# K transposed one batch ahead, P*V late in each step, and the last batch by head groups, in a cached attention kernel on Trainium2

## The chip, the cores and the metric

The kernel runs on one core of a Trainium2 chip. The core has a matrix engine (TensorE, in the profile PE, with its weight loads as PEld), VectorE (DVE), ScalarE (ACT), GpSimd (POOL) and SyncE (SP), which run side by side and wait for one another on semaphores. Data comes from HBM into SBUF by DMA, matmul results land in PSUM, which has eight banks. The metric is the time of one execution in microseconds (us) on the device. The time before is a median of 3 runs.

## What is computed

One attention block with a cache, for 32 sequences (batches) of 4 query tokens each: a query projection, attention of 32 query heads over 4 key/value heads with 2048 cached positions, and an output projection. All inputs are bf16.

```python
B, Sq, D = 32, 4, 1024
Hq, Hkv, Sk, Dh = 32, 4, 2048, 128
q = (x @ wq).reshape(B, Sq, Hq, Dh)            # heads first
k = jnp.repeat(k_cache, rep, axis=1)
v = jnp.repeat(v_cache, rep, axis=1)
scores = jnp.einsum("bhqd,bhkd->bhqk", q, k) * (Dh ** -0.5)
p = _softmax(scores, axis=-1)
o = jnp.einsum("bhqk,bhkd->bhqd", p, v)
return o.reshape(B, Sq, Hq * Dh) @ wo          # heads back beside the tokens first
```

K and V are 2048 KB each for every batch, wq and wo 8192 KB each, so some 151 MB are read from HBM.

## The kernel before

The program is written out by hand as one list of operations for each engine (`p.op`, `p.dma`), each with the names of what it waits for and the name of what it finishes. An engine runs its list strictly in that order, so an operation that waits holds up everything behind it on its engine. All loads are issued by SP, in one list too.

**Start.** x and the four pieces of wq are loaded, then K and V by batch. PE transposes x and makes the projection of all queries (L184), which ACT and DVE copy to `QT_sb`.

**A batch.** K of a batch arrives with its rows over the partitions, and its head dimension must come onto the partitions before the scores can be made. PE transposes it in eight fills of eight 128x128 blocks (`pe_fill`, L216). Each fill goes to one PSUM bank of a ring, and is copied from there to `KT_sb` by DVE (L228) or ACT (L230). PE then makes the scores of the 32 heads (`pe_qk`, L252) into `ps_s`, four banks, 32 rows for each key/value head. DVE takes the maximum (L301) and negates it (L302), ACT takes the exponential and the sum (L306), DVE the reciprocal (L311). PE transposes P in two fills (`pe_pt`, L236), DVE copies them to `PT_sb` (L243). PE multiplies P by V in 64 small matmuls (`pe_pv`, L260), 16 for each of the four head groups, each group in its own 32 columns of the array. ACT scales the result by the reciprocal into `o_sb` (L287), PE transposes it (L291), ACT copies it to `oT_sb` (L295).

**Output.** After every eighth batch PE multiplies eight batches of `oT_sb` by wo in 128 matmuls (`oproj`, L318), DVE copies the result to `y_sb` (L326), and four stores of 16 KB go out (L330), on POOL, and for the last eight batches on SP and ACT.

**Buffers.** K has two buffers (`NKB`), V three (`NVB`), K^T two (`NKTB`). The ring has three PSUM banks (`NRING`), for fills of K and P only; the fourth bank, `ps_o`, is shared by P*V, the transposed output and the output projection, which wait for one another. The load of K of batch b waits for the last fill of batch b-2 (L139), the load of V of batch b for P*V of batch b-3 (L144). V of the last batch comes in four pieces, by head group, and its P*V runs one head group after the other (L281).

**Order of a step.** K is transposed two batches ahead (`AHEAD`). Step i is: scores of i, maximum of i, P*V of i-1 and its evacuation, fills 0 and 1 of batch i+2, transpose of the output of i-1, exponential of i, fills 2 to 7 of batch i+2, in every eighth step the output projection, reciprocal of i, transposes of P of i. Steps 30 and 31 have no fills.

Of the kernel before, what the change touches and what calls it, by code (L numbers as in the profile page):

```python
# [56 lines left out]
def bass_standalone__gqa_block_cached__sampling_kernel(  # L57
# [20 lines left out]
    NKB = 2  # L78
    NVB = 3
    NKTB = 2  # L80
    AHEAD = 2
    NFILL = 8
    TB = T // NFILL
    NRING = 3
# [4 lines left out]
    ACT_FILLS = (0, 1, 5, 7)  # L89
    DVE_FILLS = (2, 3, 4, 6)  # L90
# [4 lines left out]
    with ExitStack() as es:  # L95
# [7 lines left out]
        KT_sb = sbuf("KT_sb", [128, NKTB, TV, G, R * C], BF16)  # L103
# [7 lines left out]
        y_sb = sbuf("y_sb", [128, 2, NC], BF16)  # L111
# [8 lines left out]
        ring = [ps_r[:, i, :].bitcast(BF16) for i in range(NRING)]  # L120
        ps_o = ps_r[:, 3, :]
# [54 lines left out]
        for kt in range(KT):  # L176
            p.op("pe", lambda e, kt=kt: e.transpose(
                ring[2][:, kt * 128:(kt + 1) * 128],
                x_sb.rearrange("p (c a) -> p a c", a=KT)[:, kt, :], ident[:, :]),
                ["x", "ident"], "xT" if kt == KT - 1 else None)  # L180
        p.op("dve", lambda e: e.tensor_copy(xT_sb.rearrange("p a b -> p (a b)"), ring[2]), ["xT"], "xT_evac")
# [18 lines left out]
        ring_evac = []  # L200

        def ring_slot(name):
            n = len(ring_evac)
            waits = [ring_evac[n - NRING]] if n >= NRING else [("qe", 4 + n)]
            ring_evac.append(name)
            return ring[n % NRING], waits

        slot_of = {}

        def pe_fill(b, f):  # L210
            buf, waits = ring_slot(("kt", b, f))
            slot_of["kt", b, f] = buf
            for q in range(TB):
                c, v = q // (TB // C), q % (TB // C)
                t = c * TV + f * TB // C + v
                p.op("pe", lambda e, q=q, t=t: e.transpose(  # L216
                    buf[:, q * 128:(q + 1) * 128], K_sb[:, b % NKB, t, :], ident[:, :]),
                    waits + [("k", b), "ident"] if q == 0 else [], ("fill", b, f) if q == TB - 1 else None)

        def evac(b, f):  # L220
            buf = slot_of["kt", b, f]
            waits = [("fill", b, f)]
            if b >= NKTB:
                waits.append(("qk", b - NKTB))
            dst = KT_sb[:, b % NKTB, f * TB // C:(f + 1) * TB // C, :, :].rearrange("p v g (r c) -> p (v g) r c", c=C)
            src = buf.rearrange("p (c m r) -> p m r c", c=C, r=R)
            if f in DVE_FILLS:
                p.op("dve", lambda e: e.tensor_copy(dst, src), waits, ("kt", b, f))  # L228
            else:
                p.op("act", lambda e: e.activation(dst, src, ACT.Copy), waits, ("kt", b, f))  # L230

        def pe_pt(i, f):
            buf, waits = ring_slot(("pt", i, f))
            slot_of["pt", i, f] = buf
            for q in range(8):
                p.op("pe", lambda e, q=q: e.transpose(  # L236
                    buf[:, q * 128:(q + 1) * 128], P_sb[:, (8 * f + q) * 128:(8 * f + q + 1) * 128], ident[:, :]),
                    waits + [("exp", i)] if q == 0 else [], ("ptf", i, f) if q == 7 else None)

        def evac_pt(i, f):  # L240
            buf = slot_of["pt", i, f]
            waits = [("ptf", i, f)] + ([("pv", i - 1)] if i else [])
            p.op("dve", lambda e: e.tensor_copy(  # L243
                PT_sb[:, 8 * f:8 * f + 8, :].rearrange("p t q -> p (t q)"), buf), waits, ("pt", i, f))


        def pe_qk(i):
            waits = [("kt", i, f) for f in range(NFILL)]
            waits += [("qe", j) for j in range(Hq // 4)] if i == 0 else [("exp", i - 1)]
            for c in range(4):  # L250
                for g in range(G):
                    p.op("pe", lambda e, c=c, g=g: e.matmul(  # L252
                        ps_s[32 * g:32 * (g + 1), c * 512:(c + 1) * 512],
                        lhsT=QT_sb[:, i, REP * g:REP * (g + 1), :],
                        rhs=KT_sb[:, i % NKTB, 4 * c:4 * (c + 1), g, :],
                        start=True, stop=True, tile_position=(0, 32 * g)),
                        waits, ("qk", i) if (c, g) == (3, G - 1) else None)

        def pv_mm(i, g, t, waits, done):
            p.op("pe", lambda e: e.matmul(  # L260
                ps_o[32 * g:32 * (g + 1), 0:Dh],
                lhsT=PT_sb[:, t, 32 * g:32 * (g + 1)],
                rhs=V_sb[:, i % NVB, g, t, :],
                start=(t == 0), stop=(t == TV - 1), tile_position=(0, 32 * g)), waits, done)

        def pe_pv(i):
            waits = [("pt", i, 0), ("pt", i, 1)]
            if i == 0:
                waits.append(("qe", 7))
            else:  # L270
                waits.append(("ot", i - 1))
                if i % OG == 0:
                    waits.append(("oe", i // OG - 1))
            if i < B - 1:
                waits.append(("v", i))
                for t in range(TV):
                    for g in range(G):
                        pv_mm(i, g, t, waits if t == 0 and g == 0 else [],
                              ("pv", i) if (t, g) == (TV - 1, G - 1) else None)
            else:  # L280
                for g in range(G):  # L281
                    for t in range(TV):
                        pv_mm(i, g, t, waits + [("v", i, g)] if t == 0 else [],
                              ("pv", i) if (t, g) == (TV - 1, G - 1) else None)

        def o_evac(i):
            p.op("act", lambda e: e.activation(o_sb[:, :], ps_o[:, 0:Dh], ACT.Copy, scale=rinv[:, i:i + 1]),  # L287
                 [("pv", i), ("rinv", i)] + ([("oT", i - 1)] if i else []), ("o", i))

        def pe_ot(i):  # L290
            p.op("pe", lambda e: e.transpose(ps_o[:, 0:64].bitcast(BF16), o_sb[:, :], ident[:, :]),  # L291
                 [("o", i)], ("oT", i))

        def ot_evac(i):
            p.op("act", lambda e: e.activation(  # L295
                oT_sb[:, :, i * Sq:(i + 1) * Sq],
                ps_o[:, 0:64].bitcast(BF16).rearrange("p (h s) -> p h s", s=Sq), ACT.Copy),
# [16 lines left out]
        def oproj(n):  # L314
            waits = [("wo", c) for c in range(4)] + [("ot", OG * n + OG - 1)]
            for h in range(Hq):
                for j in range(4):
                    p.op("pe", lambda e, h=h, j=j: e.matmul(  # L318
                        ps_o[32 * j:32 * (j + 1), 0:NC],
# [3 lines left out]
                        waits if (h, j) == (0, 0) else [], ("op", n) if (h, j) == (Hq - 1, 3) else None)  # L323

        def oproj_out(n):
            p.op("dve", lambda e: e.tensor_copy(y_sb[:, n % 2, :], ps_o[:, 0:NC]),  # L326
                 [("op", n)] + ([("out", n - 2, j) for j in range(4)] if n >= 2 else []), ("oe", n))
            for j in range(4):
                p.dma("act" if n == NOG - 1 and j % 2 else "sp" if n == NOG - 1 else "pool",
                      lambda e, j=j: e.dma_start(  # L330
                          out_flat[32 * n:32 * (n + 1), NC * j:NC * (j + 1)], y_sb[32 * j:32 * (j + 1), n % 2, :]),
                      [("oe", n)], ("out", n, j), f"s_o{n}{j}")

        for b in range(AHEAD):
            for f in range(NFILL):
                pe_fill(b, f)
                evac(b, f)
        for i in range(B):
            nb = i + AHEAD
            more = nb < B  # L340
# [5 lines left out]
            if more:  # L346
                for f in (0, 1):
                    pe_fill(nb, f)
                    evac(nb, f)
            if i >= 1:  # L350
                pe_ot(i - 1)
                ot_evac(i - 1)
            softmax_exp(i)
            if more:
                for f in range(2, NFILL):
                    pe_fill(nb, f)
                    evac(nb, f)
            if i >= 1 and i % OG == 0:
                oproj(i // OG - 1)
                oproj_out(i // OG - 1)  # L360
            softmax_rinv(i)
# [3 lines left out]
        pe_pv(B - 1)  # L365
        o_evac(B - 1)
        pe_ot(B - 1)
        ot_evac(B - 1)
        oproj(NOG - 1)
        oproj_out(NOG - 1)  # L370

# [55 lines left out]
```

## Time and profile before

| | us |
|---|---|
| time, median of 3 runs | 399.6 |
| lowest and highest run | 398.33, 401.64 |
| the profiled execution, its own time | 398.7 |
| its span, from the first to the last instruction | 396.9 |

The granted clock of TensorE was 0.951 of full speed on average in that execution. The time of an execution is a little longer than its span; durations below are from the span. In the profile, L12 stands for line 12 of the kernel, and a row of a group names engine, line, operation, the tile written and the tile read. "Idle before" is time in which the engine had nothing to run, with the engine or transfer that ended it. The chain of work that ended last is followed back from the last instruction: it shows which waits mattered. The table of stretches gives the busy time of each engine, the granted clock, the share of time in which the 16 DMA engines were busy (it can come out a little over 1) and the rate in GB/s.

### The profile page before, as it was taken

The numbers are of one execution on the slowest core, as the hardware profiler recorded it, in microseconds if no ns is written. First come the engines' busy times: TensorE is split into PE (matmuls) and PEld (weight loads), VectorE is DVE, ScalarE is ACT, GpSimd is POOL, SyncE is SP. The second block draws the span as 40 slices with busy tenths as digits, with TensorE's granted clock in tenths as the row PEclk, the third lists the DMA queues.
The fourth block names the chain that finished last, engine by engine and source line by source line (L and its number), as shares of the span: only waits on it lengthen the run. The fifth ranks groups of instructions, "written<-read, shape, count | busy, mean of one in ns | idle before, by whom it ended". The sixth has DMA issues, their size and how long they took to land.

```text
span 396.9 us, 12651 instructions
## 1 busy us (share of the span) xinstructions
PE 285.8 (72%) x5928; PEld 229.8 (58%) x5928; DVE 274.5 (69%) x297; ACT 207.7 (52%) x261; POOL 6.7 (2%) x18
## 2 busy tenths in 40 slices
PE   2967688466374878887777787877767878876565
PEld 2956466446364656665555575755555756655454
DVE  0017899375383984998888867988888589987520
ACT  1016677245154663676656646766666657666320
POOL 0000000000000002000000010000000010000000
PEclk9999999787888999999999999999999999999858
DMA  8999999999999999999999999999999999999400
GB/s 330 433 423 418 390 408 395 414 409 396 413 412 418 416 418 409 422 415 419 414 414 417 416 417 387 424 414 417 417 418 416 419 400 391 418 418 404 165 0 9
DMA packets 27059, 152.32 MB, mean 384 GB/s; under 512 B 1472, under 2 KB 1792, under 8 KB 22400
## 3 DMA queue, kind: packets, MB, share of 16 engines
q1 hardware_dynamic: 26528, 151.29, 93.5%
q8 instruction: 46, 0.75, 0.8%
q0 software_dynamic: 384, 0.20, 0.2%
q10 hardware_dynamic: 96, 0.03, 0.0%
q14 instruction: 5, 0.04, 0.0%
HBM read 151.26 MB, written 0.26 MB: 382 GB/s over the span
## 4 chain that ended last, share of the span: by engine, by line
DMA 51%; DVE 23%; PE 21%; issue 2%; ACT 1%; SPq 1%
DMA K_sb<-in_k_cache_dram 51%; DVE KT_sb L228 18%; PE ps_r L216 9%; DVE mx L301 4%; PE ps_r L318 4%; PE ps_r L236 3%; PE ps_s L252 3%; PE ps_r L260 2%; ACT P_sb L306 1%; SPq L133 0%; DVE negmx L302 0%; PE ps_r L291 0%; DVE PT_sb L243 0%; DVE y_sb L326 0%; SPq L130 0%
## 5 line engine op out<-in xcount | busy, mean ns | idle before, releaser
L216 PE MATMUL ps_r<-ident,K_sb 128*128 128x128 bf16 x2048 | 150.5, 227 | 86.6 <-DMA K_sb<-in_k_cache_dram 44.1
L216 PEld LDWEIGHTS ps_r<-ident,K_sb 128*128 128x128 bf16 x2048 | 123.7, 101 | 112.4 <-issue 39.1
L228 DVE COPY KT_sb<-ps_r 128x1024 bf16<-128x1024 bf16 x128 | 147.7, 1216 | 53.1 <-PE ps_r L216 53.1
L230 ACT ACTIVATE KT_sb<-ps_r 128x1024 bf16<-128x1024 bf16 x128 | 127.9, 1026 | 67.6 <-PE ps_r L216 67.5
L301 DVE TENSOR_REDUCE mx<-ps_s 128x1 f32<-128x2048 f32 x32 | 73.3, 2292 | 10.1 <-PE ps_s L252 9.6
L306 ACT ACTIVATE P_sb<-ps_s,negmx 128x2048 bf16<-128x2048 f32 x32 | 63.4, 1980 | 1.3 <-DVE negmx L302 1.3
L287 ACT ACTIVATE o_sb<-ps_r,rinv 128x128 bf16<-128x128 f32 x32 | 11.8, 367 | 84.9 <-PE ps_r L260 84.9
L236 PE MATMUL ps_r<-ident,P_sb 128*128 128x128 bf16 x512 | 40.1, 226 | 6.6 <-ACT P_sb L306 6.2
L243 DVE COPY PT_sb<-ps_r 128x1024 bf16<-128x1024 bf16 x64 | 42.2, 690 | 3.1 <-PE ps_r L236 2.2
L260 PEld LDWEIGHTS ps_r<-V_sb,PT_sb 128*32 128x32 bf16 x2048 | 33.8, 98 | 12.1 <-DVE PT_sb L243 10.6
L260 PE MATMUL ps_r<-V_sb,PT_sb 128*32 128x128 bf16 x2048 | 38.9, 222 | 1.8 <-issue 1.0
L236 PEld LDWEIGHTS ps_r<-ident,P_sb 128*128 128x128 bf16 x512 | 30.4, 100 | 13.4 <-ACT P_sb L306 6.4
L252 PE MATMUL ps_s<-KT_sb,QT_sb 128*32 128x512 bf16 x512 | 34.1, 387 | 0.0
L252 PEld LDWEIGHTS ps_s<-KT_sb,QT_sb 128*32 128x32 bf16 x512 | 10.8, 97 | 10.7 <-issue 0.7
L195 DVE CAST QT_sb<-ps_r 128x512 bf16<-128x512 f32 x2 | 1.3, 686 | 22.6 <-PE ps_r L184 22.6
L326 DVE CAST y_sb<-ps_r 128x256 bf16<-128x256 f32 x4 | 1.7, 425 | 20.2 <-PE ps_r L318 20.2
L318 PE MATMUL ps_r<-w_sb,oT_sb 128*32 128x256 bf16 x512 | 14.8, 273 | 0.4 <-ACT oT_sb L295 0.4
L184 PE MATMUL ps_s<-P_sb,w_sb 128*128 128x128 bf16 x128 | 9.8, 237 | 7.1 <-DMA w_sb<-in_wq_dram 7.1
L197 ACT ACTIVATE QT_sb<-ps_r 128x512 bf16<-128x512 f32 x2 | 1.1, 594 | 26.1 <-PE ps_r L184 26.1
L318 PEld LDWEIGHTS ps_r<-w_sb,oT_sb 128*32 128x32 bf16 x512 | 13.2, 97 | 1.3 <-ACT oT_sb L295 0.5
L184 PEld LDWEIGHTS ps_s<-P_sb,w_sb 128*128 128x128 bf16 x128 | 8.6, 107 | 7.7 <-issue 4.4
L330 POOL DMA_DIRECT2D out_dram<-y_sb x12 | 6.0, 507 | 312.4 <-DVE rinv L311 312.4
(20 smaller groups left out, 61.4 us busy)
## 6 DMA issues: line engine op xcount, KB each, us to landing
K_sb<-in_k_cache_dram SPq DMA_DIRECT2D x32, 2048.0 KB, 14.6
V_sb<-in_v_cache_dram SPq DMA_DIRECT2D x31, 2048.0 KB, 19.3
w_sb<-in_wq_dram SPq DMA_DIRECT2D x4, 2048.0 KB, 14.1
w_sb<-in_wo_dram SPq DMA_DIRECT2D x4, 2048.0 KB, 23.6
V_sb<-in_v_cache_dram SPq DMA_DIRECT2D x4, 512.0 KB, 14.6
P_sb<-in_x_dram SPq DMA_DIRECT2D x1, 256.0 KB, 2.7
out_dram<-y_sb POOLq DMA_DIRECT2D x12, 16.0 KB, 6.9
out_dram<-y_sb SPq DMA_DIRECT2D x2, 16.0 KB, 1.7
```

The lines of the kernel that those rows point to most:

```text
L184: p.op("pe", lambda e, kt=kt, h=h: e.matmul(ps_q(h), lhsT=w_sb[:, kt, h * Dh:(h + 1) * Dh], rhs=xT_sb[:, kt, :], start=(kt == 0 and h % 4 ...
L216: p.op("pe", lambda e, q=q, t=t: e.transpose(buf[:, q * 128:(q + 1) * 128], K_sb[:, b % NKB, t, :], ident[:, :]), waits + [("k", b), "iden ...
L228: p.op("dve", lambda e: e.tensor_copy(dst, src), waits, ("kt", b, f))
L230: p.op("act", lambda e: e.activation(dst, src, ACT.Copy), waits, ("kt", b, f))
L236: p.op("pe", lambda e, q=q: e.transpose(buf[:, q * 128:(q + 1) * 128], P_sb[:, (8 * f + q) * 128:(8 * f + q + 1) * 128], ident[:, :]), wai ...
L243: p.op("dve", lambda e: e.tensor_copy(PT_sb[:, 8 * f:8 * f + 8, :].rearrange("p t q -> p (t q)"), buf), waits, ("pt", i, f))
L252: p.op("pe", lambda e, c=c, g=g: e.matmul(ps_s[32 * g:32 * (g + 1), c * 512:(c + 1) * 512], lhsT=QT_sb[:, i, REP * g:REP * (g + 1), :], rh ...
L260: p.op("pe", lambda e: e.matmul(ps_o[32 * g:32 * (g + 1), 0:Dh], lhsT=PT_sb[:, t, 32 * g:32 * (g + 1)], rhs=V_sb[:, i % NVB, g, t, :], sta ...
L287: p.op("act", lambda e: e.activation(o_sb[:, :], ps_o[:, 0:Dh], ACT.Copy, scale=rinv[:, i:i + 1]), [("pv", i), ("rinv", i)] + ([("oT", i - ...
L301: p.op("dve", lambda e: e.tensor_reduce(mx[:, i:i + 1], ps_s[:, :], AX.X, ALU.max), [("qk", i)], ("mx", i))
L306: p.op("act", lambda e: e.activation(P_sb[:, :], ps_s[:, :], ACT.Exp, bias=negmx[:, i:i + 1], scale=scale, accum_out=ssum[:, i:i + 1]), [( ...
L318: p.op("pe", lambda e, h=h, j=j: e.matmul(ps_o[32 * j:32 * (j + 1), 0:NC], lhsT=oT_sb[:, h, 32 * n:32 * (n + 1)], rhs=wo_sb[:, h, NC * j:N ...
```

## The change

* K^T has one buffer, K has three, and K is transposed one batch ahead: the load of K of batch b waits for the last fill of batch b-3. Loads begin with K of 0, 1 and 2, then V of 0; from there K of b+2 stands ahead of V of b.
* The ring has all four banks, and P*V, the transposed output and the output projection take their turn in it. A turn waits for the evacuation of what used its bank four turns ago. DVE copies fills 2, 3, 5 and 7 (before 2, 3, 4 and 6), ACT the others.
* A step runs in another order: scores of i, maximum, transposed output of i-2, the output projection in every eighth step, fills 0 and 1 of i+1, exponential, fills 2 to 7 of i+1, reciprocal, P*V of i-1 and its evacuation, transposes of P of i.
* The last batch runs P*V of its first three head groups interleaved, then of the fourth; evacuates, transposes and projects 24 heads, then 8; and its projection goes to `ps_s`.
* `y_sb` has a place for each of the four groups of eight batches. Stores of the first three groups are issued on SP at the end of its list, ahead of those of the last group.

```diff
-    NKB = 2
+    NKB = 3
-    NKTB = 2
-    AHEAD = 2
-    NRING = 3
+    NRING = 4
-    ACT_FILLS = (0, 1, 5, 7)
-    DVE_FILLS = (2, 3, 4, 6)
+    DVE_FILLS = (2, 3, 5, 7)
...
-        load_v(0)
-        load_k(2)
-        nk = 3
-        for b in range(1, B):
-            if nk < B:
-                load_k(nk)
-                nk += 1
+        for b in range(B):
+            if b + 2 < B:
+                load_k(b + 2)
             load_v(b)
...
+        freed = [("qe", 4 + n) for n in range(NRING)]
+
+        def slot(free):
+            n = len(freed)
+            freed.append(free)
+            return ring[n % NRING], [freed[n - NRING]]
...
-            waits = [("fill", b, f)]
-            if b >= NKTB:
-                waits.append(("qk", b - NKTB))
+            waits = [("fill", b, f)] + ([("qk", b - 1)] if b else [])
...
         def pe_pv(i):
-            waits = [("pt", i, 0), ("pt", i, 1)]
...
+            buf, waits = slot(("o", i))
+            slot_of["o", i] = buf
+            waits = waits + [("pt", i, 0), ("pt", i, 1), ("v", i)]
+            for t in range(TV):
                 for g in range(G):
...
+                    pv_mm(buf, i, g, t, waits if t == 0 and g == 0 else [],
+                          ("pv", i) if (t, g) == (TV - 1, G - 1) else None)
...
+        for f in range(NFILL):
+            pe_fill(0, f)
+            evac(0, f)
         for i in range(B):
             pe_qk(i)
             softmax_max(i)
+            if i >= 2:
+                pe_ot(i - 2)
+                ot_evac(i - 2)
+                if i % OG == 1 and i > 1:
+                    oproj(i // OG - 1)
+            if i + 1 < B:
+                for f in (0, 1):
+                    pe_fill(i + 1, f)
+                    evac(i + 1, f)
+            softmax_exp(i)
+            if i + 1 < B:
+                for f in range(2, NFILL):
+                    pe_fill(i + 1, f)
+                    evac(i + 1, f)
+            softmax_rinv(i)
             if i >= 1:
                 pe_pv(i - 1)
                 o_evac(i - 1)
...
             for f in range(2):
                 pe_pt(i, f)
                 evac_pt(i, f)
...
+        L = B - 1
+        pe_ot(L - 1)
+        ot_evac(L - 1)
+        o_l, waits = slot(None)
+        waits = waits + [("pt", L, 0), ("pt", L, 1)]
+        for t in range(TV):
+            for g in range(3):
+                pv_mm(o_l, L, g, t, waits + [("v", L, k) for k in range(3)] if t == 0 and g == 0 else [],
+                      ("pva", L) if (t, g) == (TV - 1, 2) else None)
+        for t in range(TV):
+            pv_mm(o_l, L, 3, t, [("v", L, 3)] if t == 0 else [], ("pv", L) if t == TV - 1 else None)
...
+        oproj_mm(y_l, n, range(24), ["ota", ("ot", L - 1)], None)
...
+        oproj_mm(y_l, n, range(24, 32), ["otb"], ("op", n))
+        oproj_evac(y_l, n)
+        for m in range(NOG - 1):
+            oproj_out(m, ("sp",))
+        oproj_out(n, ("sp", "act"))
```

More of the change, by code (lines that the diff above doesn't have):

```diff
@@ L119, in bass_standalone__gqa_block_cached__sampling_kernel @@
         ps_r = es.enter_context(nc.psum_tensor("ps_r", [128, 4, 512], F32))
-        ring = [ps_r[:, i, :].bitcast(BF16) for i in range(NRING)]
-        ps_o = ps_r[:, 3, :]
+        ring = [ps_r[:, i, :] for i in range(NRING)]
         def ps_q(h):
@@ L311, in softmax_rinv, with oproj_mm @@
             p.op("dve", lambda e: e.reciprocal(rinv[:, i:i + 1], ssum[:, i:i + 1]), [("exp", i)], ("rinv", i))
-        def oproj(n):
-            waits = [("wo", c) for c in range(4)] + [("ot", OG * n + OG - 1)]
-            for h in range(Hq):
+        def oproj_mm(buf, n, heads, waits, done):
+            for h in heads:
                 for j in range(4):
                     p.op("pe", lambda e, h=h, j=j: e.matmul(
-                        ps_o[32 * j:32 * (j + 1), 0:NC],
+                        buf[32 * j:32 * (j + 1), 0:NC],
                         lhsT=oT_sb[:, h, 32 * n:32 * (n + 1)],
@@ L334, in bass_standalone__gqa_block_cached__sampling_kernel, with oproj, oproj_evac @@
[L334 to L337, printed above, removed]
+                        waits if (h, j) == (heads[0], 0) else [], done if (h, j) == (heads[-1], 3) else None)
+        def oproj(n):
+            buf, waits = slot(("oe", n))
+            oproj_mm(buf, n, range(Hq), waits + [("wo", c) for c in range(4)] + [("ot", OG * n + OG - 1)], ("op", n))
+            oproj_evac(buf, n)
+        def oproj_evac(buf, n):
+            p.op("dve", lambda e: e.tensor_copy(y_sb[:, n, :], buf[:, 0:NC]), [("op", n)], ("oe", n))
@@ L338, in bass_standalone__gqa_block_cached__sampling_kernel, with oproj_out @@
+        def oproj_out(n, engines):
+            for j in range(4):
+                p.dma(engines[j % len(engines)], lambda e, j=j: e.dma_start(
+                    out_flat[32 * n:32 * (n + 1), NC * j:NC * (j + 1)], y_sb[32 * j:32 * (j + 1), n, :]),
+                    [("oe", n)], ("out", n, j), f"s_o{n}{j}")
+        for f in range(NFILL):
+            pe_fill(0, f)
+            evac(0, f)
         for i in range(B):
-            nb = i + AHEAD
-            more = nb < B
             pe_qk(i)
@@ L364, in bass_standalone__gqa_block_cached__sampling_kernel @@
                 evac_pt(i, f)
[L365 to L370, printed above, removed]
+        L = B - 1
[9 more added lines that the diff above has]
+            pv_mm(o_l, L, 3, t, [("v", L, 3)] if t == 0 else [], ("pv", L) if t == TV - 1 else None)
+        p.op("act", lambda e: e.activation(o_sb[0:96, :], o_l[0:96, 0:Dh], ACT.Copy, scale=rinv[0:96, L:L + 1]),
+             [("pva", L), ("rinv", L), ("oT", L - 1)], "oa")
+        p.op("act", lambda e: e.activation(o_sb[96:128, :], o_l[96:128, 0:Dh], ACT.Copy, scale=rinv[96:128, L:L + 1]),
+             [("pv", L)], "ob")
+        ta, waits = slot(None)
+        ta = ta.bitcast(BF16)
+        p.op("pe", lambda e: e.transpose(ta[:, 0:96], o_sb[0:96, :], ident[0:96, 0:96]), waits + ["oa"], "oTa")
+        p.op("dve", lambda e: e.tensor_copy(
+            oT_sb[:, 0:24, L * Sq:(L + 1) * Sq], ta[:, 0:96].rearrange("p (h s) -> p h s", s=Sq)), ["oTa"], "ota")
+        y_l = ps_s[:, 0:512]
+        n = NOG - 1
+        oproj_mm(y_l, n, range(24), ["ota", ("ot", L - 1)], None)
+        tb, waits = slot(None)
+        tb = tb.bitcast(BF16)
+        p.op("pe", lambda e: e.transpose(tb[:, 0:32], o_sb[96:128, :], ident[96:128, 96:128]), waits + ["ob"], "oTb")
+        p.op("dve", lambda e: e.tensor_copy(
+            oT_sb[:, 24:32, L * Sq:(L + 1) * Sq], tb[:, 0:32].rearrange("p (h s) -> p h s", s=Sq)), ["oTb"], "otb")
+        oproj_mm(y_l, n, range(24, 32), ["otb"], ("op", n))
[3 more added lines that the diff above has]
+        oproj_out(n, ("sp", "act"))
         names = list(p.ENGINES) + sorted({s for s in p.dma_count})
```

87 lines of the change are left out of this document (21 added, 66 removed).

## The prediction

> **What bounds the kernel now.** I read the page's head, then its row of GB/s by slice, then the chain of work that ended last by engine.
>
> ```profile
> PE 285.8 (72%) x5928; PEld 229.8 (58%) x5928; DVE 274.5 (69%) x297; ACT 207.7 (52%) x261; POOL 6.7 (2%) x18
> GB/s 330 433 423 418 390 408 395 414 409 396 413 412 418 416 418 409 422 415 419 414 414 417 416 417 387 424 414 417 417 418 416 419 400 391 418 418 404 165 0 9
> DMA 51%; DVE 23%; PE 21%; issue 2%; ACT 1%; SPq 1%
> K_sb<-in_k_cache_dram SPq DMA_DIRECT2D x32, 2048.0 KB, 14.6
> V_sb<-in_v_cache_dram SPq DMA_DIRECT2D x31, 2048.0 KB, 19.3
> ```
>
> No engine is full, yet the DMA rate stands near 417 GB/s from the first slices to the 37th of 40. A batch is one K and one V load, 2 x 2048 KB = 4.19 MB, so at 417 GB/s it takes 10.06 us. The engines need less. In the order-of-time listing of PE after an output projection, where PE waits for no load, one step follows another like this (start, length, engine, line, tile):
>
> ```profile
> 326.98 1.22 PE L236 MATMUL ps_r<-ident,P_sb 128*128 128x128 bf16 x16
> 335.68 1.23 PE L236 MATMUL ps_r<-ident,P_sb 128*128 128x128 bf16 x16
> ```
>
> That is 8.70 us a step. So the kernel has two parts: a stream of loads that sets the pace, and a tail after the last K has landed. The table of stretches (stretch, length, PE, PEld, DVE, ACT, POOL busy, granted clock, DMA share, GB/s) shows how full the stream is:
>
> ```profile
> 60.00:120.00 60.00, 37.37 (x729) 30.98 (x726) 37.20 (x40) 26.22 (x34) 0.00 (x0) 0.83 1.03 406
> 120.00:240.00 120.00, 91.34 (x2041) 72.29 (x2042) 93.40 (x101) 70.11 (x89) 4.05 (x8) 0.99 1.02 417
> 240.00:260.00 20.00, 16.99 (x357) 13.34 (x355) 18.39 (x20) 15.29 (x20) 0.00 (x0) 1.00 1.00 405
> 325.00:330.00 5.00, 4.18 (x113) 3.04 (x112) 4.66 (x7) 2.95 (x4) 0.00 (x0) 1.00 0.89 331
> ```
>
> It is full but for two dents, each a step or so behind an output projection (3.7 us of PE). The first costs 20 x (417-405)/417 = 0.6 us, the second 5 x (417-331)/417 = 1.0 us. The tail is the end of the chain in order of time (start, length, what):
>
> ```profile
> 344.53 14.69 DMA K_sb<-in_k_cache_dram
> 359.35 1.05 PE ps_r L216 x16
> 367.27 2.30 DVE mx L301
> 369.78 2.07 ACT P_sb L306 x2
> 371.89 1.89 PE ps_r L236 x16
> 373.78 1.61 PE ps_s L252 x12
> 375.42 2.30 DVE mx L301
> 377.93 2.07 ACT P_sb L306 x2
> 380.04 1.90 PE ps_r L236 x16
> 381.97 0.70 DVE PT_sb L243
> 382.71 5.68 PE ps_r L260 x61
> 388.42 0.38 ACT o_sb L287
> 389.11 0.28 ACT oT_sb L295
> 389.44 3.71 PE ps_r L318 x128
> 393.17 0.42 DVE y_sb L326
> ```
>
> The last K lands at 344.53 + 14.69 = 359.2; call this T. The span ends at 396.9, so the tail is 37.7 us. It holds the transposes of the last K (for batch 31), a whole softmax of batch 30, a whole softmax of batch 31, P*V, and the output. The second softmax starts only because K was transposed two batches ahead: batch 30's scores come after batch 31's K.
>
> **The change, part by part: the stream.** Bytes and load order stay, but for V of batch 0, which goes behind K of batch 2. With three K buffers, the load of K(b) waits for the transposes of batch b-3 instead of b-2. At the end of step i, with K(i+1) transposed and V(i-1) used, four loads may stand issued behind it: K(i+2), V(i), K(i+3), V(i+1), which is 4 x 5.03 = 20 us. Before, a K load landed 14.6 us after its issue. P*V moves to the end of its step, so V(i+2) is issued later within the step, but behind that 20 us queue it is hidden. Both dents should fill: I take 0.6 + 1.0 = 1.6 us. Bounds: nothing, or 4.5 us if the weak start (390 and 395 GB/s in slices 5 and 7) and the uneven end (165 in the 38th) also level out. A loss of 1 us is left open, since the issue order on SP changes.
>
> **The step.** What could undo this is a longer step. The ACT and PE rows of batch 30's step give the lengths:
>
> ```profile
> 361.97 1.98 ACT L306 ACTIVATE P_sb<-ps_s,negmx 128x2048 bf16<-128x2048 f32 x1
> 363.92 1.04 ACT L230 ACTIVATE KT_sb<-ps_r 128x1024 bf16<-128x1024 bf16 x1
> 365.01 1.22 PE L236 MATMUL ps_r<-ident,P_sb 128*128 128x128 bf16 x16
> 366.17 1.05 PE L252 MATMUL ps_s<-KT_sb,QT_sb 128*32 128x512 bf16 x16
> 367.04 1.06 PE L260 MATMUL ps_r<-V_sb,PT_sb 128*32 128x128 bf16 x64
> ```
>
> The new ring gives 12 slots a step (oT, eight fills, o, two P^T) over four banks, so P*V takes the bank of fill 4, which ACT copies out after the exponential. The new loop is: scores to maximum 1.10 (366.17 to 367.27), maximum to exponential 2.51 (to 369.78), exponential to fill 4's copy 1.95, the copy 1.04, the hand-over 0.15, P*V 1.0, P^T to scores 1.16. The sum is 8.9 us, against 8.70 before and DVE's 274.5/32 = 8.6. It stays under 10.06, so the stream still paces the kernel. P*V also waits for V(i-1), which follows K(i+1) by one transfer (5.0 us); fill 4 is copied 5.75 us after the K landing, so V is hidden with 0.7 us to spare. The projections now stand on PE ahead of the fills and push those back by some 3.6 us; at 10.06 - 8.9 = 1.2 us a step that is made good in three or four steps. The last one is at step 25, and T belongs to step 30. The 20 us queue covers the lag. The second K^T buffer goes without cost, as PE does the scores of i before the fills of i+1 anyway.
>
> **The tail, from T.** In step 30 the first fill starts 0.14 after T, the exponential follows ACT's first two copies, and fill 4's copy ends 363.92 + 1.04 - 359.21 = 5.75 after T. P*V of batch 29 follows to 6.9, P^T to 8.05, where the scores of 31 start (before, scores of 30 started at 7.0). Then 1.10 to the maximum, 2.51 to the exponential, 2.11 to P^T (369.78 to 371.89), 2.63 to its copies' end (380.04 to 382.67): 16.4. P*V of 30 and its transpose fit in the gaps. The last P*V before went head group by head group: 64 in 5.68, or 0.0887 each. Now three groups interleave: 16 rounds bounded by 1.42 (a round costs what one does) and 4.26 (no overlap). The interleaved P*V row (1.06 for 64, 0.066 a round at clock 1.00) is nearer the low end; doubled for the half clock it gives 2.1, so I take 1.8. The fourth group alone costs 16 x 0.0887 = 1.42. That ends at 19.7 with its hand-over. Evacuating the first 96 rows hides behind group four, the last 32 behind the projection. A transpose and a copy follow: 0.24 + 0.36; the copy has no DVE row, and between the 0.28 of ACT's oT copy and the 0.42 of y's I take 0.28 and 0.08 of hand-over. Projection of 24 heads: 96/128 x 3.71 = 2.78. A second transpose and copy: 0.6. Eight heads: 0.93. Copy of y 0.44. From there to the end as before, 396.9 - 393.59 = 3.31. Sum 28.3.
>
> The clock must be added. The last matmul ahead of the last softmax, and PE's busy time, its granted clock, DMA share and GB/s in single microseconds at the end:
>
> ```profile
> 376.73 0.23 PE L291 MATMUL ps_r<-ident,o_sb 128*128 128x128 bf16 x1 [0.48 <-ACT o_sb L287]
> ...
> 371.00:372.00 1.00, 0.11 (x2) 0.78 0.48 188
> 374.00:375.00 1.00, 1.00 (x16) 0.52 0.00 0
> 378.00:379.00 1.00, 0.00 (x0) 0.69 0.00 0
> 387.00:388.00 1.00, 1.00 (x14) 0.50 0.00 0
> 388.00:389.00 1.00, 0.54 (x5) 0.69 0.00 0
> ```
>
> The clock fell to 0.5 between 378 and 379, some 2 us after that last matmul, and before that between 371 and 372. It came back 3.2 us after work began at 371.9, and 8.6 us after it began at 380.04, just in time for the old projection. The new P*V is 2.4 us shorter, so the projection may begin cold. Work begins at T+13.8; with the first delay the clock is full throughout, with the second until T+22.4 cold, which is 2.3 us of the projection at half rate, or 1.2 us lost. I take 0.9 from nearer the second. Bounds: 0, and 3.7 (the whole projection at half rate).
> The Trainium skill (TensorE: Matmul & The Clock Gate, Part 1) says the clock rises after about 3.4 us of sustained work, on free-running windows, and falls after an idle one. The trace agrees on the rise at 375 and shows the fall earlier. By that rule the rise would come in the first full window behind P*V's start, T+19.9 to T+23.3, for an estimated loss of about 0.8 us.
>
> **Stores.** Twelve 16 KB stores move from POOL to SP's queue at the end.
>
> ```profile
> 357.31 2.64 SPq L149 DMA_DIRECT2D V_sb<-in_v_cache_dram  x4
> 393.62 1.09 SPq L330 DMA_DIRECT2D out_dram<-y_sb  x2
> DMA to landing us min/median/max: 13.3/14.6/15.7
> ```
>
> At 1.09/2 = 0.55 each they hold SP 6.5 us, from about T-1 (the last V issue waits for P*V of 28 in step 29) to T+6; the last batch's stores come at T+25, so 0. The third row is the four V pieces of the last batch: landed by 357.31 + 15.7 = 373.0, T+13.8, ahead of the P*V at 16.4.
>
> **Sum.** The tail is 28.3 + 0.9 = 29.2 against 37.7, 8.5 less; with the stream's 1.6 that is 10.1. The profiled execution took 398.7 (span 396.9 and 1.8 around it) and would take 388.6. It lies 0.9 below the median of 399.6, so the median would be 389.5.
>
> **Rivals.**
> (a) The stream gains nothing: its slowest queues were busy anyway. The 38th slice at less than half rate speaks for it, since some queues end late; the dents speak against it. 399.6 - 8.5 = 391.1.
> (b) The projection runs cold to its end, as the last P*V did: 3.7 instead of 0.9, 392.3. The 8.6 us of cold work speaks for it; against it, PE now runs with gaps of only 0.4 us from T+16.4.
> (c) Slower: PE loses its clock in the steady steps. The late P*V leaves PE waiting for fill 4's copy, and at half clock the loop grows: P^T from 1.22 to 1.89, scores from 1.05 to 1.61, P*V from 1.0 to 2.0, together 2.2, to 11.1 us. From step 8 on that costs 24 x 1.0 = 25 us, some 414. It decides where a step passes 10.06 + 10/24 = 10.5. Against it: clock 0.99 in 120 to 240 with the same work, and cold steps only in the stretch where loads of Wo stretch the step.
>
> **How the numbers follow.** Chances: forecast 0.64, (a) 0.15, (b) 0.13, (c) 0.05, others 0.03. A measurement of this kernel can tell about 1%, 4 us, from no change. The forecast, (a) and (b) lie below 395.6, and I leave a little of their tails above it: faster 0.90, within 1% 0.05, slower 0.05. The range goes from 385.5 (stream 4.5, clock 0: 389.5 - 2.9 - 0.9, a little in) to 394.5 ((a) and (b) together, 394).
>
> **What would show it.** In the changed profile: K's last landing at 357 to 359 after the span's start; between it and the end 29 us; one maximum of scores behind it, not two; no dent in GB/s after the second and third projection; steps of 10.06 us with PE waiting for K; P*V of the last batch near 3.2 us; clock back to 1.00 during the projection. Wrong if a K wait is gone from the steady steps, if the last K lands after 360, or if the projection takes over 5 us.

## The result and the profile after

The changed kernel took 387.25 us (median of 3 runs, 387.23 to 387.38) against 399.6: a ratio of 0.969, with a 95% interval of 0.962 to 0.975. The forecast was 389.5, with a range of 385.5 to 394.5. The profiled execution took 387.23, its span 385.4.

From the page of the changed kernel: span, GB/s by slice, the chain that ended last by engine, and the issues of K and V (size of one, microseconds from issue to landing).

```profile
span 385.4 us, 12595 instructions
GB/s 328 432 432 416 418 417 398 413 410 395 413 409 409 419 416 414 419 413 418 417 419 417 417 414 417 416 416 411 417 417 417 418 420 415 417 418 410 375 143 9
DMA 59%; PE 17%; ACT 13%; DVE 7%; issue 2%; SPq 1%
K_sb<-in_k_cache_dram SPq DMA_DIRECT2D x32, 2048.0 KB, 25.4
V_sb<-in_v_cache_dram SPq DMA_DIRECT2D x31, 2048.0 KB, 27.3
```

The dents behind the projections are gone, and K waits in a queue of 25 us where it was 15. The table of stretches (columns as before the change) says the same of the two dents, and shows the end of the loads:

```profile
240.00:260.00 20.00, 15.95 (x343) 12.56 (x341) 19.05 (x21) 14.30 (x17) 0.00 (x0) 1.00 1.02 416
325.00:330.00 5.00, 4.82 (x105) 3.79 (x93) 4.69 (x7) 2.81 (x6) 0.00 (x0) 1.00 0.99 406
...
365.00:370.00 5.00, 3.28 (x102) 2.14 (x90) 3.73 (x4) 0.90 (x3) 0.00 (x0) 1.00 0.57 220
370.00:375.00 5.00, 2.81 (x43) 2.38 (x46) 1.55 (x3) 2.33 (x4) 0.00 (x0) 0.59 0.32 117
```

405 became 416 and 331 became 406. From 365 to 372 the loads run at about half rate (186 to 268 GB/s by single microseconds). That stretch has grown: before the change it went from 369 to 373. The last piece of V shows why. A load lands in sixteen shares, each a step of its semaphore: eight of them are there by 366.2, the other eight come from 371.9 to 373.9.

The tail of the chain, in order of time:

```profile
332.92 25.64 DMA K_sb<-in_k_cache_dram
...
364.12 1.08 PE ps_r L248 x64
...
366.20 1.01 PE ps_s L240 x16
367.23 2.30 DVE mx L280
369.74 2.07 ACT P_sb L285 x2
371.85 1.90 PE ps_r L225 x16
374.53 3.16 PE ps_r L248 x49
378.18 2.80 PE ps_s L296 x96
381.37 1.08 PE ps_s L296 x32
```

The last K lands at 332.92 + 25.64 = 358.6, where it was 359.2. One maximum follows it, where there were two. The tail is 385.4 - 358.6 = 26.8 us, where it was 37.7. So of the 11.5 us by which the span shrank, 10.9 came from the tail and 0.6 from the stream of loads.

### The profile page after: what moved, and what is told of

It reads as the page before. It is cut to its first block, busy times and chain, and to the rows that moved or that the text cites. A ratio compares the mean times of both kernels' runs of the same rounds, so it can differ in the third digit from the quotient of the medians.

```text
span 385.4 us, 12595 instructions
## 1 busy us (share of the span) xinstructions
PE 280.9 (73%) x5929; PEld 229.5 (60%) x5929; DVE 274.1 (71%) x299; ACT 208.5 (54%) x261; POOL 0.7 (0%) x6
## 4 chain that ended last, share of the span: by engine, by line
DMA 59%; PE 17%; ACT 13%; DVE 7%; issue 2%; SPq 1%
DMA K_sb<-in_k_cache_dram 59%; ACT KT_sb L219 7%; ACT P_sb L285 6%; DVE KT_sb L217 4%; PE ps_r L207 4%; PE ps_r L248 3%; PE ps_r L296 3%; PE ps_r L225 3%; PE ps_s L240 3%; DVE mx L280 2%; PE ps_s L296 1%; DVE PT_sb L231 0%; SPq L129 0%; PE ps_r L271 0%; ACT oT_sb L275 0%
## 5 line engine op out<-in xcount | busy, mean ns | idle before, releaser
L207 PE MATMUL ps_r<-ident,K_sb 128*128 128x128 bf16 x2048 | 142.6, 229 | 66.0 <-DMA K_sb<-in_k_cache_dram 40.8
L207 PEld LDWEIGHTS ps_r<-ident,K_sb 128*128 128x128 bf16 x2048 | 125.7, 103 | 82.2 <-DMA K_sb<-in_k_cache_dram 41.9
L219 ACT ACTIVATE KT_sb<-ps_r 128x1024 bf16<-128x1024 bf16 x128 | 124.5, 1025 | 72.1 <-PE ps_r L207 72.0
L248 PE MATMUL ps_r<-V_sb,PT_sb 128*32 128x128 bf16 x2048 | 36.7, 223 | 17.2 <-ACT KT_sb L219 12.8
L248 PEld LDWEIGHTS ps_r<-V_sb,PT_sb 128*32 128x32 bf16 x2048 | 31.0, 98 | 22.7 <-ACT KT_sb L219 19.4
L275 ACT ACTIVATE oT_sb<-ps_r 128x128 bf16<-128x128 bf16 x31 | 8.6, 277 | 55.6 <-PE ps_r L271 55.6
L225 PE MATMUL ps_r<-ident,P_sb 128*128 128x128 bf16 x512 | 35.1, 223 | 1.8 <-ACT P_sb L285 1.4
L187 DVE CAST QT_sb<-ps_r 128x512 bf16<-128x512 f32 x2 | 1.3, 686 | 22.4 <-PE ps_r L176 22.4
L296 PE MATMUL ps_r<-w_sb,oT_sb 128*32 128x256 bf16 x384 | 11.5, 273 | 2.6 <-issue 1.4
L296 PEld LDWEIGHTS ps_r<-w_sb,oT_sb 128*32 128x32 bf16 x384 | 10.0, 97 | 3.7 <-issue 2.5
L271 PEld LDWEIGHTS ps_r<-ident,o_sb 128*128 128x128 bf16 x31 | 3.0, 98 | 12.7 <-issue 12.7
```

The source lines that it names most:

```text
L207: p.op("pe", lambda e, q=q, t=t: e.transpose(buf[:, q * 128:(q + 1) * 128], K_sb[:, b % NKB, t, :], ident[:, :]), waits + [("k", b), "iden ...
L225: p.op("pe", lambda e, q=q: e.transpose(buf[:, q * 128:(q + 1) * 128], P_sb[:, (8 * f + q) * 128:(8 * f + q + 1) * 128], ident[:, :]), wai ...
L248: p.op("pe", lambda e: e.matmul(buf[32 * g:32 * (g + 1), 0:Dh], lhsT=PT_sb[:, t, 32 * g:32 * (g + 1)], rhs=V_sb[:, i % NVB, g, t, :], star ...
L296: p.op("pe", lambda e, h=h, j=j: e.matmul(buf[32 * j:32 * (j + 1), 0:NC], lhsT=oT_sb[:, h, 32 * n:32 * (n + 1)], rhs=wo_sb[:, h, NC * j:NC ...
```

## The experiments

Each is the changed kernel with one edit. The changed kernel itself gave 387.25, and 387.11 (385.62 to 388.12) when it was run again beside the last of them; the kernel before gave medians of 397.4 to 398.3 on the four chips of these runs, so between chips a difference of a microsecond is not sure by the times alone. "T" is the landing of the last K, in the profile of the run.

**K transposed two batches ahead again**

```diff
-    NKB = 3
+    NKB = 2
+    NKTB = 2
...
-            if i + 1 < B:
+            if i + 2 < B:
                 for f in (0, 1):
-                    pe_fill(i + 1, f)
-                    evac(i + 1, f)
+                    pe_fill(i + 2, f)
+                    evac(i + 2, f)
...
```

> The changed kernel with K transposed two batches ahead again (two K^T buffers, two K buffers); P*V late, ring of four, last batch by head groups stay. Theory (the tail is one softmax shorter because only one batch is transposed ahead): the last K lands within 1 us of 358.5, two maxima of scores follow it instead of one, and the span grows by one score-to-score round of the old tail, 366.2 to 373.7, so 7.5 us: about 395. Rival (the gain came from the other parts, and the order of the tail hides the extra softmax): under 2 us longer, below 389.

Measured: 397.16 us (396.24 to 397.27), 9.9 more, and level with the kernel before (ratio to it 0.998, interval 0.996 to 1.000). The maxima and the last P*V, from its listing in order of time:

```profile
369.09 2.29 DVE L281 TENSOR_REDUCE mx<-ps_s 128x1 f32<-128x2048 f32 x1 [0.15 <-PE ps_s L241]
...
376.93 2.29 DVE L281 TENSOR_REDUCE mx<-ps_s 128x1 f32<-128x2048 f32 x1 [1.15 <-PE ps_s L241]
...
384.22 3.15 PE L249 MATMUL ps_r<-V_sb,PT_sb 128*32 128x128 bf16 x64 [0.67 <-DVE PT_sb L232]
```

Two maxima follow T again, 7.84 us apart. T itself is 360.4, 1.8 later, so the tail grew by 395.2 - 360.4 - 26.8 = 8.0. The theory holds for the tail. The 1.8 goes with the K buffers, which this edit also takes back: the next run, with that alone, moves T by 2.3.

**Two K buffers instead of three**

```diff
-    NKB = 3
+    NKB = 2
```

> The changed kernel with two K buffers instead of three, nothing else. Step of the prediction (the deeper queue fills dents and moves the last K forward): a K load lands some 15 us after its issue again instead of 25, dents come back behind the projections, the last K lands 1 to 2 us later and the time grows as much. Rival (the last eight of sixteen shares of each load set the pace, and were never starved in the kernel before either): the first eight shares of the last K land some 5 us later, the last share within 0.7 us of 358.6, and the time stays within 1 us.

Measured: 389.6 us (388.56 to 391.82), T at 360.9. That is 2.3 later on both counts, a little over the 1 to 2 expected, and the rival's bound of 1 us falls. But the place isn't the one that the prediction's step names. GB/s by slice in this run:

```profile
GB/s 333 429 429 268 422 409 403 409 404 407 411 395 413 420 415 421 418 414 419 415 415 420 416 416 404 411 413 419 411 422 413 421 390 408 397 420 414 405 220 8
```

The fourth slice stands at 268. The mean rate loses 9.7 x (417-268)/417 = 3.5 us there: K of 2 waits for the fills of batch 0, and V of 0 waits behind it on SP. Later dents are small. I therefore tried the old order of the first loads:

**Two K buffers, and V of 0 ahead of K of 2**

```diff
-    NKB = 3
+    NKB = 2
...
+        load_v(0)
+        load_k(2)
-        for b in range(B):
+        for b in range(1, B):
```

> The run with two K buffers, but with V of 0 loaded ahead of K of 2, as before the change. In the run with two K buffers the fourth of 40 slices stood at 268 GB/s: K of 2 waited on SP for the fills of 0 with V of 0 behind it. Theory (the third buffer pays at the start alone, since in the steady steps the last eight shares of each load set the pace): the fourth slice is over 380 GB/s, the last share of the last K lands within 0.8 us of 358.6, against 360.9, and the time is within 1 us of 387.3. Rival (the depth of the queue counts in every step): the last share stays near 360.5, the time at 389 or more.

Measured: 388.63 us (386.38 to 389.47), T at 360.8. Neither theory came out as written. The fourth slice was whole, but the gap only moved by one step, to where K of 3 waits for the fills of batch 1 (stretch from 40 to 50 us of this run):

```profile
40.00:50.00 10.00, 7.31 (x112) 5.58 (x110) 9.93 (x13) 7.55 (x8) 0.00 (x0) 1.00 0.80 313
```

By the last share of the load that lands near 50 us this run is 1.7 behind the changed kernel, and at T 2.2. The last share alone swings by a microsecond from load to load. By the mean of the eight shares that land last, this run is 2.2 behind near 50 us and 2.5 at the last K, and the run before it 3.6 and 3.2. So the third buffer earns its 2 to 3 us in the first 50 us, and nothing that can be seen after that. The theory had the place right, but its edit moved the gap and did not close it. One batch ahead with two buffers makes the start worse than in the kernel before (that load 1.4 later, T 1.6 later), and the third buffer pays that back.

**Where the stream's gain went.** Each of these loads raises its semaphore sixteen times, once for each share that lands. These are the times of the first, eighth, ninth and last share of the last K, read from the semaphore's updates in the traces:

```
                              1st    8th    9th    16th
before                      354.0  354.5  357.4  359.2
changed                     348.9  351.0  356.7  358.6
two K buffers               355.7  357.0  360.2  360.9
two K buffers, V of 0 first 355.3  356.7  359.0  360.8
few key blocks in P*V       349.1  351.1  353.8  355.6
```

In the changed kernel the first eight shares land 5.1 to 3.5 us earlier than before, the last only 0.6. K counts as landed with its last share. The filled dents went to the eight early shares, and the eight late ones set the pace: behind each of the two dents of the kernel before, the first share comes 6.8 and 6.9 us after that of the load before it, the ninth only 5.1 and 5.2, where 5.0 is the rule. What makes them late? The page lists instruction fetches among the DMA queues; the next run takes some away.

**P*V of batches 0 to 27 with one of sixteen key blocks.** This leaves out 15/16 of those products; it takes instructions from TensorE and nothing from the loads.

```diff
...
-            for t in range(TV):
+            nt = 1 if i < 28 else TV
+            for t in range(nt):
...
```

> The changed kernel with one of sixteen key blocks in P*V of batches 0 to 27, which leaves out 3360 of TensorE's 11858 instructions and so some 13 of the 46 instruction fetches of 16 KB that run on the same DMA engines as the loads. Theory (a fetch takes 1.05 us of one DMA engine, and they fall on the eight engines that are late): some two fetches fewer on each of these, the spread of the shares of the last K falls from 9.7 to about 7, its last share lands 1.3 to 2.6 us earlier, and the time falls as much. Rival (these engines are slower for another reason): last share and time within 0.7 us.

Measured: 384.42 us (384.31 to 384.91), 2.8 less. The queue of instruction fetches (packets, MB, share of 16 engines) in the changed kernel and then in this one, and the first fill of batch 31 in this one:

```profile
q8 instruction: 46, 0.75, 0.8%
```

```profile
q8 instruction: 33, 0.54, 0.6%
```

```profile
355.67 2.41 PE L207 MATMUL ps_r<-ident,K_sb 128*128 128x128 bf16 x40 [1.29 <-DMA K_sb<-in_k_cache_dram]
```

The fill starts 2.9 us earlier, the last share lands 3.0 earlier, the first eight shares land as before (table above). Thirteen fetches of 16 KB are gone, and only the eight late shares gained. Times and shares moved as the theory says, but by more than its 1.3 to 2.6.

The semaphore of the changed kernel shows each fetch. Ahead of the first one, at 17.8, the sixteen shares of a load land within 0.6 us. In the load that ends at 19.9 one share comes 1.4 us behind the rest. K at 34.4 has two such shares (the second fetch is at 29.3), V at 44.4 three (39.6), V at 54.7 four (49.9), K at 59.6 five (57.2). With few key blocks the fifth fetch comes at 61.6, and the fifth late share with the load at 64.6. When all eight have had their turn, a new round begins: the gap of the ninth share to that of the load before is 6.3 to 6.5 us instead of 5.0 after the fetches at 160.4, 275.4 and 335.9. So a fetch, itself mostly 1.0 to 1.1 us long, puts one share 1.3 to 1.5 us behind. Ahead of the last K come 42 fetches in the changed kernel, five rounds of eight and two more, and two shares land last, at 358.5 and 358.6. With few key blocks there are 29, three rounds and five, and five shares land last. So the last share is spared two fetches, 2.6 to 3.0 us by the steps above, and 3.0 was measured; the expectation had counted the length of the fetch alone.

So the fetches slow the loads on eight of the sixteen DMA engines, if a share stands for an engine; the trace doesn't name the engines. The rival (slower for another reason) falls for these eight. Two of the early shares fall some 1.7 us behind as well, in both runs; why was not tried.
The Trainium skill (Runtime: NRT & Kernel Launch, Instruction fetch mechanics) says that an engine's instructions come in blocks of 16 KiB over a DMA queue of its own, at a cost that is mostly hidden. The trace agrees on the blocks. The cost to the loads, 2.8 us for 13 fetches, is not hidden here.

**Taking bytes from the late engines: K of batch 16 in sixteen transfers**

```diff
+            if b == 16:
+                src = k_cache[b].rearrange("g (r t) d -> (g r) t d", r=R)
+                for j in range(16):
+                    p.dma("sp", lambda e, j=j: e.dma_start(
+                        K_sb[8 * j:8 * (j + 1), b % NKB, :, :], src[8 * j:8 * (j + 1)]),
...
```

> The changed kernel with K of batch 16 loaded as sixteen transfers of 8 partitions each, so that each may run on eight of the sixteen DMA engines alone. Theory (eight engines run some 10 us ahead at the end, and the other eight set the pace of all K and V): if the eight that get the transfers are the ones ahead, the shares of the last K land together, its last share some 4 to 5 us earlier (354), and the time falls by 4 to 5 us; if they are the late ones, the last share comes 5 us later and the time grows by 5 us. Rival (the spread of the shares does not set the pace): within 1 us.

Measured: 406.12 us (404.7 to 408.17), T at 375.9, so neither the theory nor the rival. In a second form each transfer took every sixteenth partition (`K_sb[j:128:16, ...]`).

> As the run with sixteen transfers of 8 partitions for K of batch 16, but each takes every sixteenth partition instead of 8 neighbours. Theory (that run lost 18 us because 8 neighbouring partitions take what one transfer writes through too narrow a way, each 128 KB taking some 3 us): the sixteen transfers now land within some 10 us, and what is left is the balance between the sixteen DMA engines: if the eight used are the early ones, the last K's last share lands 4 to 5 us earlier than 358.6, the time falls as much; if they are the late ones, both grow by 5 us. Rival (small transfers as such cost the 18 us): again over 400.

Measured: 403.91 us (402.67 to 407.34). In both, this K landed some 40 us after its first issue (180.3 to 223.3, and 179.8 to 220.0), where a whole K takes 25. Each transfer raised the semaphore nine times and not sixteen; by eights of the other shares most landed 1.0 to 1.7 us after the one before, and from 195 to 220 the rate stood at 202 to 239 GB/s, about half. So the neighbouring partitions were not the cause. Loading this K in sixteen transfers cost the time, but which part of it did, their size or the few engines that they ran on, is not shown. Whether the engines can be balanced stays open.

**P*V ahead of the fills**

```diff
+            if i >= 1:
+                pe_pv(i - 1)
+                o_evac(i - 1)
             if i + 1 < B:
                 for f in (0, 1):
...
-            if i >= 1:
-                pe_pv(i - 1)
-                o_evac(i - 1)
```

> The changed kernel with P*V of i-1 and its evacuation moved ahead of the fills of i+1, as the old order had it. Theory (V of i-1 comes one transfer behind K of i+1, and PE runs in order, so the fills stand behind a wait for V): the fills of batch 31 start at 364.9 instead of 358.6, the scores of 31 at 371.8 instead of 366.1, the time grows by 5.5 us; the steady steps stay at 10.06 us. Rival (P*V has no place that matters, as the stream sets the pace): within 1 us.

Measured: 392.61 us (392.45 to 392.82), 5.4 more. PE in order of time, P*V of 29, the first fills of 31, the scores of 31:

```profile
363.87 1.08 PE L248 MATMUL ps_r<-V_sb,PT_sb 128*32 128x128 bf16 x64 [1.35 <-DMA V_sb<-in_v_cache_dram]
364.88 2.41 PE L207 MATMUL ps_r<-ident,K_sb 128*128 128x128 bf16 x40
...
371.39 1.05 PE L240 MATMUL ps_s<-KT_sb,QT_sb 128*32 128x512 bf16 x16
```

T is 358.6 as in the changed kernel, but the fills start at 364.9, behind V's landing. Each number is within 0.5 us of what was expected. The late place of P*V costs nothing in the steady steps and is worth 5.4 us at the end.

**The last batch as before**: P*V group by group, one evacuation, one transpose, one projection.

```diff
-        for t in range(TV):
-            for g in range(3):
...
+        for g in range(G):
+            for t in range(TV):
+                pv_mm(o_l, L, g, t, waits + [("v", L, g)] if t == 0 else [],
...
```

> The changed kernel with the last batch's P*V group by group, one evacuation, one transpose and one projection, as before. Theory: P*V takes up to 5.7 us instead of 3.1, less what the clock gives back when it rises some 3 us into it; the work from P*V to the copy of y stays at 4.8; so 1.9 to 2.5 us longer. Rival (V's last piece, landing at about 374, holds both orders alike): within 0.7 us.

Measured: 387.95 us (387.48 to 388.98), 0.7 more. That is at the rival's edge and within what two chips can differ by, while its profiled execution (388.98, the slowest) is 1.8 above that of the changed kernel, just under the theory:

```profile
374.62 4.82 PE L248 MATMUL ps_r<-V_sb,PT_sb 128*32 128x128 bf16 x64 [0.68 <-DVE PT_sb L231]
```

4.82 us of P*V against 3.16, so 1.7 there. It waits for P^T's copy and not for V, which is not the rival's reason. The size, 0.7 to 1.8 us, stays open.

**Stores back on POOL**

```diff
             oproj_evac(buf, n)
+            oproj_out(n, ("pool",))
...
-        for m in range(NOG - 1):
-            oproj_out(m, ("sp",))
```

> The changed kernel with the stores of the first three groups issued on POOL when their copy is ready, as before. Theory (stores are off the path in both places): within 1 us. Rival (the stores on SP's queue stand between the end and the last stores, or POOL's stores disturb the loads): more than 1 us either way.

Measured: 387.52 us (387.36 to 387.75). The stores are off the path in both places.

**PE kept busy ahead of the last products**

```diff
+        def warm(name, n):
+            buf, waits = slot(("warm", name))
+            buf = buf.bitcast(BF16)
+            for q in range(n):
+                p.op("pe", lambda e, q=q: e.transpose(
+                    buf[:, (q % 8) * 128:(q % 8 + 1) * 128], ident[:, :], ident[:, :]),
+                    waits if q == 0 else [], ("warm", name) if q == n - 1 else None)
...
+                if i == B - 1:
+                    warm(0, 16)
...
+            if i == B - 1:
+                warm(1, 20)
...
+        warm(2, 10)
```

> The changed kernel with 46 idle transposes of the identity on PE in the gaps of the last step: 16 behind the transposed output of 29, 20 behind P*V of 30, 10 ahead of the last P*V. Theory (the last P^T and P*V run at half clock only because PE idles ahead of them): the clock stays 1.00 from 367 to the end, P^T takes 1.2 instead of 1.9 us, P*V some 2.1 instead of 3.2, the projection is unchanged, and the time falls by about 1.6 us. Rival (the last piece of V, landing at 373.9, or the stream holds the end): the clock rises but the time stays within 0.5 us.

Measured: 385.93 us (385.3 to 386.21), 1.2 to 1.3 less than the changed kernel's two medians, and the fastest version here that computes everything. The ranges overlap by a little; the spans of the profiled executions, 384.1 against 385.4 and 384.7, go the same way. First the changed kernel by single microseconds (PE busy, clock, DMA share, GB/s), then this run's P^T and P*V:

```profile
371.00:372.00 1.00, 0.15 (x2) 0.50 0.51 186
376.00:377.00 1.00, 1.00 (x24) 0.50 0.00 0
377.00:378.00 1.00, 0.88 (x8) 0.63 0.00 0
378.00:379.00 1.00, 0.82 (x32) 1.00 0.00 0
```

```profile
371.72 1.07 PE L225 MATMUL ps_r<-ident,P_sb 128*128 128x128 bf16 x16
...
373.72 1.15 PE L248 MATMUL ps_r<-V_sb,PT_sb 128*32 128x128 bf16 x53 [0.32 <-DVE PT_sb L231]
375.25 0.79 PE L248 MATMUL ps_r<-V_sb,PT_sb 128*32 128x128 bf16 x11 [0.39 <-issue]
```

Without the idle transposes the clock is at half from 371 until P*V ends, in this execution. With them it was 1.00 from 365 to 382, P^T took 1.07 instead of 1.90 and P*V, from start to end, 2.3 instead of 3.2. The 0.39 in the middle is a wait that no other engine ended. The fall and the rise are partly chance: in each of these traces the changes of the clock lie a multiple of 3.41 us apart, and where they fall against the last products differs from one execution to the next. In the second profiled execution of the changed kernel the clock fell at 373.4 and rose at 376.8, and P*V began 0.7 us earlier.

## Why the prediction was right, and where not

Direction, place and size came out: forecast 10.1 us less, measured 12.35 by the medians and 11.5 by the profiled executions. The difference of the two is the three runs of the kernel before, whose median was 0.9 above its profiled execution; side by side on one chip the medians were 398.26 and 387.11, 11.15 apart. The prediction was right for the tail and wrong for the stream, and the tail's terms were too cautious; that the two errors, 1.0 and 2.4 us, go against each other is luck.

*The stream.* Forecast 1.6, measured 0.6. The dents filled as forecast, so the step that failed is the one that turned a filled dent into an earlier K. Mean GB/s counts sixteen engines; a load lands with its last share, and the late eight shares are held up by instruction fetches. Rival (a), that the slowest queues were busy anyway, was largely right, and its argument (less than half rate in the 38th slice) was the row to weigh more. It was not wholly right: with two buffers the late shares do starve, in the first 50 us.

*The step.* Forecast 8.9 us where nothing waits for loads. Two P*V of the chain after the third projection:

```profile
315.73 1.08 PE ps_r L248 x64
...
324.37 1.08 PE ps_r L248 x64
```

8.64 us, below 10.06 and below the old 8.70. The projections' push was made good, and PE waits for K again from 337 on. Rival (c) needed 10.5 and never came near; the clock from 130 to 370 was 1.00. (In the second profiled execution it fell three times in that stretch, for 3.4 us each, and T was 358.6 all the same.)

*V behind K.* Forecast 0.7 us to spare. In the changed kernel P*V of 29 starts at 364.1, behind ACT's copy, with V landed at 363.7: 0.4 to spare. The run with P*V early shows what stood behind it.

*The tail, 29.2 forecast, 26.8 measured.* To the end of P^T's copies: 16.4 forecast, 374.5 - 358.6 = 15.9 measured. The last P*V: 3.2 forecast, 3.16 measured. The projection: 2.78 forecast, 2.80 measured, at full clock. The term that was mis-sized is the clock: 0.9 was added for a cold projection, and the clock rose at 377.7, as P*V ended and 0.4 ahead of the projection, so 0. That is T + 19.1, where the prediction had T + 22.4, or T + 19.9 at the earliest behind the start of P*V. In the second profiled execution the projection ran at full clock too, so rival (b) falls for these two; that it can't happen is not shown, since the rise is partly chance. Two delays were misread: by the rows shown, 0.52 and 0.69, the clock came back 3.1 us after 371.9, not 3.2, and fell 1.4 us after the last matmul, not some 2. What the clock does cost is in P^T and P*V, where the prediction had it inside the rows it took. From the copy of y to the end 3.31 was taken from before; it is 385.4 - 382.9 = 2.5.

*One batch ahead.* This carries the result: 8.0 us of the tail by its own run, where the score-to-score round was 7.5. It isn't the only part that is needed: one batch ahead with P*V in its old place loses 5.4 of it, and with two K buffers some 2 more.

*What was nearly missed.* The last piece of V landed at 373.9, so T + 15.3 and not T + 13.8: the late shares again. P^T is ready at 374.5. P*V begins with three head groups, whose pieces had landed by 372.6, so a tail up to 1.9 us shorter ahead of P*V would not have waited there. The fourth piece, landed at 373.9, was needed only when the last quarter began, at some 376.4.

## What to carry to other kernels

When a stream of loads sets the pace, cost a reordering by what still has to run after the last load, and count whole rounds of dependent steps there; that is where 10.9 of 11.5 us came from. Ask whether a filled gap in the mean rate moves the last share of a load, or only the shares that were early. If an operation waits for a transfer that comes after the one its neighbours wait for, put it behind them in its engine's order, even where the steady step shows no difference.

## What the runs showed of the hardware

* Most instruction fetches of 16 KB took 1.0 to 1.1 us, and each put one of sixteen shares of the loads 1.3 to 1.5 us behind, eight of them in turn. By the last K the eight late shares were some 8 us behind the others; 13 fetches fewer made the kernel 2.8 us faster.
* A load of 2 MB as sixteen transfers of 8 partitions landed some 40 us after its first issue, where one transfer of 128 partitions takes 25 in the same queue, and the rate of all loads meanwhile stood at about half.
* In these traces the changes of TensorE's granted clock lie multiples of 3.41 us apart. 46 idle transposes in the gaps of the last step kept it at 1.00, and the last P^T and P*V took 1.07 and 2.3 us instead of 1.90 and 3.2.
* The span ended 2.5 to 2.9 us after the copy of y in the runs with all stores on SP and ACT, and 3.3 and 3.4 in the two profiled ones with earlier stores on POOL. Why was not tried.
